# Windowed attention and a softplus FFN: three key chunks folded to two, weights and v in three bfloat16 parts, transposed by DMA, q and k laid transposed

## The chip, the cores and the metric

The kernel runs on one core of one Trainium2 chip. The metric is the device time of one launch in microseconds (us); lower is better. Three runs of the kernel before gave a median of 1070.63 us (1069.97 to 1071.72). The engines are named as in the profile: PE is TensorE (PEld its weight loads), DVE VectorE, ACT ScalarE, POOL GpSimd, SP SyncE, which issues the DMAs.

## The reference, cut to what matters

```python
# q, k, v: (8, 8, 576, 64) float32; w_in (512, 2048), w_out (2048, 512) float64
scores = (1 / sqrt(64)) * q @ k.transpose(0, 1, 3, 2)
rel = pos[:, None] - pos[None, :]
scores = where((rel >= 0) & (rel < 64), scores, -1e9)
attn = exp(scores - max(scores))
attn = attn / (sum(attn) + 1e-9)
x = (attn @ v) as 4608 tokens x 512        # heads side by side
h = x @ w_in
out = ((maximum(h, 0) + log1p(exp(-abs(h)))) @ w_out) as float32
```

Each query sees itself and the 63 keys before it in its own sequence. With 128 queries in a tile, the keys in question are 192: 64 before the tile and the tile's own 128.

## The kernel before, in words

The 4608 tokens are worked in 12 blocks of 384 tokens (TB), which the code counts by g; each block has 3 query tiles of 128 (j) and 4 pairs of heads (hp). One call of `attention(g, hp)` handles one pair of heads of one block and leaves its part of x, transposed, in a high and a low float32r part. The feed-forward part (FFN) handles a block in 16 steps (f), one for each 128 of the 2048 hidden columns: `ffn_up` makes 12 matmuls into a PSUM bank `ps_h` (L450), ACT computes softplus' log term in three instructions (absolute value, exponential, logarithm: L454, L455, L456), DVE adds the positive part (L458) and splits the result into a high and a low part (`g0` at L460, `g1` at L461), and `ffn_down` makes 9 matmuls from them into three banks `ps_o` (L471). Products are made in three passes: high times high, high times low, low times high. In `ffn_down` the first two matmuls of each three read `g0`, the third reads `g1`.

The float64 weights are cut into float32r parts on the chip by `load_w` and `float64_split` (L153 to L174), once, while the first blocks are worked.

For blocks of g >= 2 one call of attention does this. It loads q, k and v in rows. It cuts q and k into three bfloat16 parts (L309 to L313), two in each 128-wide row, which the DMA transposes into `tr` (L314). Per query tile it makes 6 score matmuls of 192 keys (L334), 18 for a pair, adds the mask and takes the row's extreme on DVE (L342), takes the exponential with its sum on ACT (L345), and divides on DVE (L352, L353, L358). PE transposes the 256-wide rows `p_t` in float32 against an identity (L379, L380), two transposes a tile and head. ACT and DVE bring them out of PSUM in two parts (L385, L386). Eight matmuls a head multiply them by v (L427), also in two parts, and ACT and DVE collect `xf` (L431, L432) and split it into x (L139 on DVE, L140 on POOL).

The blocks g = 0 and 1 (`by_pe`) take another way: PE transposes q and k, too, all in float32.

The order of the work is an event list (L497 to L527). Step n of the FFN puts `ffn_up` at place 2n + 0.5 and `ffn_down` at 2n + 3.5, so that one step's down product comes after the next step's up product. The stages of `attention`, which is a generator, get places by the tables STG0, STG2 and STG, the bases BASE, PACE, SH and SHP; from block 3 on a pair of heads comes every 8 places, that is every 4 FFN steps. From place 100 on PE executes in the order of that list. The instructions of ACT, DVE, POOL and SP are ordered by the scheduler at build time; each engine then works its own list strictly from top to bottom.

Of the kernel before, what the change touches and what calls it, by code (L numbers as in the profile page):

```python
# [15 lines left out]
P = 128  # L16
# [3 lines left out]
BIG = 1.0e9  # L20

# [3 lines left out]
PACE = (5, 5, 4)  # L25
STG0 = (-8, 1, 3, 4, 5, 7, 8, 9, 10)
STG2 = (-8, 0, 2, 3, 4, 6, 7, 8, 9)
STG = (-13, -5, 0, 0, 3, 5, 7, 8, 11)
SH, SHP = -5, 8
# [7 lines left out]
def window_attention_softplus_ffn(  # L37
    ctx: ExitStack,
    tc: tile.TileContext,
    q: bass.AP,  # L40
    k: bass.AP,
    v: bass.AP,
    w_in: bass.AP,
    w_out: bass.AP,
    out: bass.AP,
):
# [35 lines left out]
    ident = cpool.tile([P, P], F32, name="ident")  # L82
    make_identity(nc, ident)


    W = WIN + P
    mask = cpool.tile([P, W], BF16, name="mask")
    nc.gpsimd.memset(mask, 0.0)
    nc.gpsimd.affine_select(
        out=mask, in_=mask, pattern=[[1, W]], compare_op=ALU.is_gt, fill=BIG, base=0, channel_multiplier=-1  # L90
    )
    nc.gpsimd.affine_select(
        out=mask, in_=mask, pattern=[[-1, W]], compare_op=ALU.is_ge, fill=BIG, base=WIN, channel_multiplier=1
    )

    mask_b = cpool.tile([P, W], BF16, name="mask_b")
    nc.gpsimd.tensor_copy(mask_b, mask)
    nc.gpsimd.memset(mask_b[WIN:P, 0:P], BIG)

    p_ts = [[cpool.tile([P, NJ, 2 * P], F32, name=f"p_t{i}{hh}") for hh in range(2)] for i in range(2)]  # L100


    NQ, NKB = 2 * NJ, 2 * (NJ + 1)
    NT2 = 2 * (NQ + NKB)
    for t in p_ts[0] + p_ts[1]:
        nc.gpsimd.memset(t[:, :, 0:WIN], 0.0)

# [4 lines left out]
    SPARE = 4 * DM * 4  # L112
# [13 lines left out]
    kbd_s = [spare(k, [P, 2, WIN + TB], F32, f"kbd{k}") for k in range(2)]  # L126
    for t in kbd_s:
        nc.gpsimd.memset(t[D:P, 0, :], 0.0)
        nc.gpsimd.memset(t[0:D, 1, :], 0.0)
    v_pads = []  # L130
    for n in range(2):
        t = spare(6 + n, [P, 2, NJ + 1, 2, P], F32, f"v_pad{n}")
        nc.gpsimd.memset(t, 0.0)
        v_pads += [t[:, i, :, :, :] for i in range(2)]
# [7 lines left out]
    NK = (NJ - 1) * W + P  # L142

    def raw_tiles(f):

        ks = (5,) if f < NE else [k for k in (5,) if k >= 4] if f < NE + 4 else []
        at = f % (len(ks) + 1)
        if at == len(ks):
            return [ff.tile([P, NC, P], w_in.dtype, name="raw", bufs=2) for _ in range(2)]
        t = spare(ks[at], [P, 2, NC, P], w_in.dtype, "raws")  # L150
        return [t[:, m, :, :] for m in range(2)]

    def float64_split(dst_hi, dst_lo, src, raw, n):  # L153


        nc.sync.dma_start(raw, src)
        words = raw.bitcast(U32).rearrange("p c (n two) -> p two c n", two=2)
        low, high = words[:, 0, :, :], words[:, 1, :, :]
        w = ff.tile([P, NC, P], F32, name="osb", bufs=2)
        wb = w.bitcast(U32)  # L160
        nc.scalar.activation(w, high.bitcast(F32), AF.Abs)
        (nc.gpsimd if n < 4 else nc.vector).tensor_scalar(w, w, ZERO_HIGH, None, ALU.max)  # L162
# [3 lines left out]
        nc.scalar.copy(dst_hi, w)  # L166
        nc.gpsimd.tensor_tensor(dst_lo, w, dst_hi.bitcast(F32), ALU.subtract)

    def load_w(f):
        fs = slice(f * P, (f + 1) * P)  # L170
        raws = raw_tiles(f)
        for m, src in enumerate((w_in[:, fs].rearrange("(c p) n -> p c n", p=P), w_out[fs, :].rearrange("p (c n) -> p c n", n=P))):
            hi, lo = [weight(m, i, f).rearrange("p (c n) -> p c n", n=P) for i in range(2)]
            float64_split(hi, lo, src, raws[m], 2 * f + m)  # L174


    def pieces(t0, n):

# [378 lines left out]
```

## Time and profile before

| | |
|---|---|
| median of 3 runs | 1070.63 us |
| the profiled execution's own time | 1069.74 us |
| its span (first to last instruction) | 1067.9 us |
| granted TensorE clock, mean | 0.993 |
| instructions on PE, DVE, ACT, POOL | 6096, 2319, 1669, 217 |
| busy share of the span: PE, PEld, DVE, ACT, POOL | 96%, 87%, 74%, 61%, 21% |
| moved by DMA | 98.20 MB, 92 GB/s on average |

Instruction counts are those of the page, which shows the execution in a span of its own; the profiled execution's time is 1.8 us longer than the span. PE's matmuls are pipelined, so one matmul's listed duration is longer than what it costs in a dense row. What it costs is read from the start of one group to the start of the next in the timeline. The same holds, by some 0.1 us each, for ACT and DVE.

### The profile page before, as it was taken

To read this page: it belongs to the slowest core of one execution; us is meant where nothing else is said; L and a number is where in the kernel's file an instruction comes from. 1 tells how busy PE (TensorE), PEld (TensorE's weight loads), DVE (VectorE), ACT (ScalarE), POOL (GpSimd) and SP (SyncE) were. 2 spreads that over 40 slices of the span, in tenths; PEclk is the share of its full clock that TensorE was granted. 3 is DMA by queue.
4 is the path that set the end of the run, shared out by engine and by line. 5 is a ranking of instruction groups with operands and counts; after the bars stand their busy time and mean duration, and the time that the engine had idled before them with its cause. 6 is when DMAs were issued, how large, how long until landed. Compare 5 with 4: busy or idle time off the path is not lost.

```text
span 1067.9 us, 18172 instructions
## 1 busy us (share of the span) xinstructions
PE 1028.4 (96%) x6096; PEld 924.3 (87%) x6096; DVE 789.0 (74%) x2319; ACT 650.0 (61%) x1669; POOL 224.7 (21%) x217
## 2 busy tenths in 40 slices
PE   7797988999999999999999999999999999999998
PEld 5576867888999899999999999999999999999996
DVE  4999899866777777777777777777777777865433
ACT  6786666666665666566656666656666665655333
POOL 4354355631111111112111111111211111110000
PEclk9999998999999999999999999999999999999999
DMA  7754645255334434343344334424434533520000
GB/s 197 198 140 105 169 105 146 67 127 119 70 71 101 96 79 105 64 97 81 81 96 96 84 76 93 107 60 88 102 74 84 115 80 62 131 51 1 30 1 30
DMA packets 296222, 98.20 MB, mean 92 GB/s; under 512 B 280512, under 2 KB 288704, under 8 KB 296128
## 3 DMA queue, kind: packets, MB, share of 16 engines
q1 hardware_dynamic: 296128, 97.03, 40.0%
q8 instruction: 48, 0.79, 0.3%
q14 instruction: 46, 0.38, 0.1%
HBM read 50.07 MB, written 10.22 MB: 56 GB/s over the span
## 4 chain that ended last, share of the span: by engine, by line
PE 78%; DVE 12%; DMA 4%; ACT 3%; issue 2%; SPq 1%; POOL 0%; DVEq 0%; ACTq 0%
PE ps_h L450 32%; PE ps_o L471 31%; PE ps_a L334 5%; PE ps_a L427 4%; PE ps_a L380 2%; DMA tr<-nat 2%; PE ps_a L379 2%; DVE p_t L358 2%; DVE osb L165 2%; DVE osb L164 1%; DVE osb L162 1%; DVE p_t L342 1%; DVE osb L163 1%; SPq L198 1%; DVE u L458 1%
## 5 line engine op out<-in xcount | busy, mean ns | idle before, releaser
L450 PE MATMUL ps_h<-x,w 128*128 128x384 f32 x2304 | 458.4, 344 | 15.4 <-DVE u L458 11.8
L471 PE MATMUL ps_o<-w,g 128*128 128x512 f32 x1728 | 438.7, 397 | 6.3 <-ACT g L460 4.3
L450 PEld LDWEIGHTS ps_h<-x,w 128*128 128x128 f32 x2304 | 400.6, 189 | 27.5 <-DVE u L458 12.5
L471 PEld LDWEIGHTS ps_o<-w,g 128*128 128x128 f32 x1728 | 318.1, 188 | 65.6 <-ACT g L460 4.6
L458 DVE SCALAR_TENSOR_TENSOR u<-ps_h,u 128x384 f32<-128x384 f32 x192 | 106.0, 552 | 139.7 <-ACT u L456 139.5
L454 ACT ACTIVATE u<-ps_h 128x384 f32<-128x384 f32 x192 | 93.6, 488 | 179.4 <-PE ps_h L450 177.2
L345 ACT ACTIVATE p_t<-p_t,mn 128x192 f32<-128x192 f32 (+1 forms) x288 | 127.0, 443 | 63.5 <-DVE mn L342 63.2
L140 POOL TENSOR_TENSOR x<-xf,x 128x384 fp32r<-128x384 f32 x40 | 41.1, 1027 | 460.6 <-DVE rs L352 362.9
L358 DVE TENSOR_SCALAR p_t<-p_t,rs 128x192 f32<-128x192 f32 (+1 forms) x288 | 110.4, 429 | 2.9
L342 DVE CUSTOM_DVE_ANT_0 p_t<-ps_a,mask 128x192 f32<-128x192 f32 (+1 forms) x244 | 77.3, 343 | 46.5 <-PE ps_a L334 36.1
L455 ACT ACTIVATE u<-u 128x384 f32<-128x384 f32 x192 | 100.7, 526 | 4.1
L456 ACT ACTIVATE u<-u 128x384 f32<-128x384 f32 x192 | 100.6, 524 | 3.2
L461 DVE TENSOR_TENSOR g<-u,g 128x384 fp32r<-128x384 f32 x160 | 89.5, 559 | 3.8 <-DVE g L460 0.5
L385 ACT CAST pt<-ps_a 128x512 fp32r<-128x512 f32 (+1 forms) x144 | 59.0, 417 | 33.7 <-PE ps_a L380 21.9
L312 POOL TENSOR_TENSOR nat<-q_in,nat 128x384 bf16<-128x384 f32 x40 | 38.6, 965 | 187.8 <-ACT nat L311 152.1
L386 DVE TENSOR_TENSOR pt<-ps_a,pt 128x512 fp32r<-128x512 f32 (+1 forms) x144 | 67.9, 477 | 12.3 <-ACT pt L385 10.7
L334 PE MATMUL ps_a<-tr 128*128 128x192 bf16 (+1 forms) x720 | 74.8, 246 | 0.9 <-DVE xf L432 0.7
L460 DVE CAST g<-u 128x384 fp32r<-128x384 f32 x176 | 67.9, 386 | 5.9
L380 PE MATMUL ps_a<-ident,p_t 128*128 128x128 f32 x276 | 66.6, 276 | 1.4 <-DVE p_t L358 1.3
L427 PEld LDWEIGHTS ps_a<-pt,vt 128*128 128x128 f32 (+1 forms) x608 | 64.0, 163 | 3.9 <-issue 0.5
L427 PE MATMUL ps_a<-pt,vt 128*128 128x64 f32 (+4 forms) x608 | 64.5, 247 | 0.4 <-DVE mn L342 0.4
L431 ACT COPY xf<-ps_a 64x384 f32<-64x384 f32 x80 | 38.1, 477 | 40.3 <-PE ps_a L427 37.5
(91 smaller groups left out, 1019.3 us busy)
## 6 DMA issues: line engine op xcount, KB each, us to landing
out_dram<-raw SPq DMA_DIRECT2D x12, 512.0 KB, 3.2
q_in<-in_q_dram SPq DMA_DIRECT2D x56, 96.0 KB, 2.6
raw<-in_moe_w_in_dram SPq DMA_DIRECT2D x10, 512.0 KB, 4.2
raw<-in_moe_w_out_dram SPq DMA_DIRECT2D x10, 512.0 KB, 4.2
k_in<-in_k_dram SPq DMA_DIRECT2D x32, 128.0 KB, 3.5
v_in<-in_v_dram SPq DMA_DIRECT2D x32, 128.0 KB, 2.8
raws<-in_moe_w_in_dram SPq DMA_DIRECT2D x6, 512.0 KB, 4.2
raws<-in_moe_w_out_dram SPq DMA_DIRECT2D x6, 512.0 KB, 5.0
```

Source lines behind the costliest of these rows:

```text
L334: mm(spv[:, hh, :], tr_q[a][:, hh, j * P : (j + 1) * P], tr_k[b][:, hh, kc], start=(hh == 0 and i == 0), stop=(hh == 1 and i == 2), skip_g ...
L342: nc.vector.tensor_tensor_reduce(pv, spv[:, hh, :], m[:, c0:], 1.0, 3.0e38, ALU.add, ALU.min, mn[:, j, hh : hh + 1])
L345: nc.scalar.activation(pv, pv, AF.Exp, bias=mn[:, j, hh : hh + 1], scale=-1.0, accum_out=sm[:, j, hh : hh + 1])
L358: nc.vector.tensor_scalar(pv, pv, rs[:, jj, hh : hh + 1], None, ALU.mult)
L427: mm(av[: D if lo else P, osl], vt[:, vb, hh, : 1 if lo else 2, :], pt[hh][lo][:, psl], start=(i == 0), stop=(i == len(order) - 1), skip_g ...
L450: mm(hv, weight(0, a, f)[:, c * P : (c + 1) * P], x[b][c], start=(i_mm == 0), stop=(i_mm == 3 * NC - 1))
L454: nc.scalar.activation(u, hv, AF.Abs)
L455: nc.scalar.activation(u, u, AF.Exp, scale=-1.0)
L456: nc.scalar.activation(u, u, AF.Ln, bias=1.0)
L458: nc.vector.scalar_tensor_tensor(gf, hv, 0.0, u, ALU.max, ALU.add)
L461: (nc.vector if g >= 2 else nc.gpsimd).tensor_tensor(gt[1], gf, gt[0].bitcast(F32), ALU.subtract)
L471: mm(ops[g][j], gt[a][:, js], weight(1, b, f), start=(first and i == 0), stop=(last and i == 2),)
```

## The change

- The host lays q and k transposed (heads and dimensions in rows, tokens in columns), v by tokens, and the float64 weights by FFN step (`_layouts`). The kernel loads q and k as they are needed; all transposes of q and k go, on PE and by DMA.
- q and k are used as float32r in a high and a low part (L238 to L243). Both halves of the partitions hold the same rows; one half of q's tile carries the high part, the other the low part. A query tile takes 4 score matmuls of 192 keys (L258), 12 for a pair, in place of 18 in bfloat16.
- The scores of a tile stay 192 wide up to the mask (L265). Then the first and the third 64 columns, of which every row has at most one inside its window, are folded into one by a minimum on DVE (L271). All that follows has 128 columns: the exponentials (L275, six in a row), the division (L281, one instruction for all six), the transposes.
- For g >= 2 the attention weights are cut into three bfloat16 parts (L300, L301, L302, L306, L307), which the DMA transposes (L303, L308). PE's 12 transposes for a pair of heads and what brought them out of PSUM go. v is cut into three bfloat16 parts, too (L316 to L320). A head takes 14 matmuls of 64 or 128 columns (L367).
- g = 0 and 1 keep PE's transposes for the weights alone (L288).
- `load_w` handles both weight matrices of a step in one instruction each, 1024 columns wide.
- The stage tables are changed. From block 3 on, the stage that casts q and k for the next pair comes at the place of this pair's first score matmuls, and the stage with all six exponentials and the splits right behind the third.

FFN lines move: `ffn_up`'s matmuls from L450 to L391, its ACT lines from L454, L455, L456 to L395, L396, L397, its DVE lines from L458, L460, L461 to L399, L401, L402; `ffn_down` from L471 to L412.

ACT, the stretch of one pair of heads in the settled part of the program, before. `u` is the FFN step's softplus term, `p_t` the attention weights, `nat` the parts of q and k, `pt` the transposed weights, `xf` attention's output.

```order
L454 ACTIVATE u_6076<-ps_h_6063 128x384
L311 CAST nat_6236<-q_in_6007 128x6x64
L455 ACTIVATE u_6076<-u_6076 128x384
L311 CAST nat_6236<-k_in_6008 128x8x64
L456 ACTIVATE u_6076<-u_6076 128x384
L385 CAST pt10_6051<-ps_a_6094 128x512
L454 ACTIVATE u_6115<-ps_h_6102 128x384
L431 COPY xf_6126<-ps_a_6127 64x384
L455 ACTIVATE u_6115<-u_6115 128x384
L345 ACTIVATE p_t00_101,sm_6137<-p_t00_101,mn_6136 128x128
L345 ACTIVATE p_t01_102,sm_6137<-p_t01_102,mn_6136 128x128
L456 ACTIVATE u_6115<-u_6115 128x384
```

ACT at the same place now. `k0` and `q_hl` are the casts of k and q for the next pair, `st` holds the weights of this pair, `v12` parts of v.

```order
L316 CAST v12_6078<-v_in_5593 128x14x64
L372 COPY xf_6155<-ps_a_6224 64x384
L318 CAST v12_6078<-v_in_5593 128x14x64
L395 ACTIVATE u_6263<-ps_h_6250 128x384
L239 CAST k0_6206<-k_in_6042 128x896
L238 CAST q_hl_6205<-q_in_6041 128x768
L396 ACTIVATE u_6263<-u_6263 128x384
L275 ACTIVATE st_6195,sm_6197<-st_6195,mn_6196 128x128 x6
L397 ACTIVATE u_6263<-u_6263 128x384
L395 ACTIVATE u_6336<-ps_h_6323 128x384
```

Between a step's first and last ACT instruction stood at most two of attention's at a time here; now eight stand inside one step, the casts of k and q and all six exponentials.

DVE, before, around the same FFN step as in ACT's first piece (`mn` and `sm` are the rows' extremes and sums, `rs` the reciprocals):

```order
L352 TENSOR_SCALAR rs_6138<-sm_6137 128x2
L353 RECIPROCAL rs_6138<-rs_6138 128x2
L458 SCALAR_TENSOR_TENSOR u_6115<-ps_h_6102,u_6115 128x384
L358 TENSOR_SCALAR p_t00_101<-p_t00_101,rs_6138 128x128
L358 TENSOR_SCALAR p_t01_102<-p_t01_102,rs_6138 128x128
L460 CAST g0_6120<-u_6115 128x384
L352 TENSOR_SCALAR rs_6138<-sm_6137 128x2
L461 TENSOR_TENSOR g1_6121<-u_6115,g0_6120 128x384
```

DVE, now, around the step `u_6263` of ACT's second piece:

```order
L271 TENSOR_TENSOR st_6195<-st_6195 128x6x64
L243 TENSOR_TENSOR k1_6207<-k_in_6042,k0_6206 128x896
L240 TENSOR_TENSOR q_hl_6205<-q_in_6041,q_hl_6205 64x768
L278 TENSOR_SCALAR sm_6197<-sm_6197 128x6
L279 RECIPROCAL sm_6197<-sm_6197 128x6
L281 TENSOR_TENSOR st_6195<-st_6195,sm_6197 128x6x128
L399 SCALAR_TENSOR_TENSOR u_6263<-ps_h_6250,u_6263 128x384
L401 CAST g0_6268<-u_6263 128x384
L399 SCALAR_TENSOR_TENSOR u_6336<-ps_h_6323,u_6336 128x384
L402 TENSOR_TENSOR g1_6269<-u_6263,g0_6268 128x384
```

The step's own DVE work now stands behind the whole division, which needs the sums of all six exponentials, and its `g1` behind the next step's first DVE instruction.

On PE the order of such a stretch is now, for the four FFN steps A to D of one pair: up A, scores of tile 0, down of the step before; 14 matmuls of the second head of the pair before, scores of tile 1, up B, scores of tile 2, down A; up C, down B; up D, down C; 14 matmuls of the next head. `u_6263` above belongs to B, `u_6336` to C.

The diff, cut to its core:

```diff
-STG = (-13, -5, 0, 0, 3, 5, 7, 8, 11)
-SH, SHP = -5, 8
+STG = (-14, -8, 0, 1, 2, 3, 15, 17)
+SH, SHP = -13, 8
...
+    def load_w(f):
+        if f % 2 and f < NE + 4:
+            raw, w = spare(6, [P, 2, DM], w_words.dtype, "raws"), spare(7, [P, 2, DM], F32, "ws")
+        else:
+            raw = ff.tile([P, 2, DM], w_words.dtype, name="raw", bufs=1)
+            w = ff.tile([P, 2, DM], F32, name="osb", bufs=1)
+        nc.sync.dma_start(raw, w_words[f])
...
+        else:
+            q_in = ld.tile([P, 2, TB], F32, name="q_in")
+            k_in = ld.tile([P, 2, W - P + TB], F32, name="k_in")
+            v_in = ld.tile([P, NCH, P], F32, name="v_in")
+            ts, ks = slice(t0, t0 + TB), slice(t0 - CH, t0 + TB)
+            for half in heads:
+                nc.sync.dma_start(
+                    q_in[half, :, :], qT[c0 : c0 + P, ts].rearrange("(h d) t -> d h t", h=2)
+                )
+                nc.sync.dma_start(
+                    k_in[half, :, :], kT[c0 : c0 + P, ks].rearrange("(h d) t -> d h t", h=2)
+                )
+            for half in heads:
+                nc.sync.dma_start(v_in[half, :, :], v[ks, c0 : c0 + P].rearrange("(c p) n -> p c n", p=CH))
+        yield
         if not by_pe:
+            q_hl = att.tile([P, 2, TB], F32R, name="q_hl")
+            k_hi, k_lo = [att.tile([P, 2, W - P + TB], F32R, name=f"k{i}") for i in range(2)]
+            low = heads[1]
+            nc.scalar.copy(q_hl, q_in)
+            nc.scalar.copy(k_hi, k_in)
+            nc.vector.tensor_tensor(
+                q_hl[low, :, :], q_in[low, :, :], q_hl[low, :, :].bitcast(F32), ALU.subtract
+            )
+            nc.vector.tensor_tensor(k_lo, k_in, k_hi.bitcast(F32), ALU.subtract)
+        yield
...
+                for hh in range(2):
+                    for i, part in enumerate((k_hi, k_lo)):
+                        mm(
+                            spv[:, hh, :], q_hl[:, hh, js], part[:, hh, kc],
+                            start=(hh == 0 and i == 0), stop=(hh == 1 and i == 1), skip_group_check=True,
+                        )
...
+        sv = st.rearrange("p h j c -> p (h j) c")
+        nc.vector.tensor_tensor(sv[:, :, 0:CH], sv[:, :, 0:CH], sv[:, :, P:], ALU.min)
+        for hh in range(2):
+            for j in range(NJ):
+                i = hh * NJ + j
+                nc.scalar.activation(
+                    sv[:, i, 0:P], sv[:, i, 0:P], AF.Exp, bias=mn[:, hh, j : j + 1], scale=-1.0, accum_out=sm[:, i : i + 1]
+                )
+        nc.vector.tensor_scalar(sm, sm, 1.0e-9, None, ALU.add)
+        nc.vector.reciprocal(sm, sm)
+        pn = sv[:, :, 0:P]
+        nc.vector.tensor_tensor(pn, pn, sm.unsqueeze(2).to_broadcast([P, 2 * NJ, P]), ALU.mult)
...
+            nc.scalar.copy(part(0, 0), pv[0])
+            nc.vector.tensor_tensor(pv[0], pv[0], part(0, 0), ALU.subtract)
+            nc.scalar.copy(part(0, 1), pv[0])
+            nc.sync.dma_start(
+                tr[:, 0:n, :], nat[:, 0, :, :, :].rearrange("p n b c -> p (n b c)"), transpose=True
+            )
+            nc.gpsimd.tensor_tensor(part(1, 0), pv[0], part(0, 1), ALU.subtract)
+            nc.vector.tensor_copy(nat[:, 1, :, 1, :], nat[:, 0, :, 0, :])
+            nc.sync.dma_start(
+                tr[:, n:, :], nat[:, 1, :, :, :].rearrange("p n b c -> p (n b c)"), transpose=True
+            )
...
+            nc.scalar.copy(v12[:, :, :, 0, :], vv)
+            nc.vector.tensor_tensor(vv, vv, v12[:, :, :, 0, :], ALU.subtract)
+            nc.scalar.copy(v12[:, :, :, 1, :], vv)
+            nc.gpsimd.tensor_tensor(v13[low, :, :, :], vv[low, :, :, :], v12[low, :, :, 1, :], ALU.subtract)
+            nc.vector.tensor_copy(v13[up, :, :, :], v12[up, :, :, 0, :])
         yield
...
+            for i, (s, c, src, osl) in enumerate(passes):
                 mm(
+                    av[: D if s else P, osl], v13[:, c, hh, :] if s else v12[:, c, hh, :, :], src,
+                    start=(i == 0), stop=(i == len(passes) - 1), skip_group_check=True,
                 )
...
+def _layouts(inputs):
+    got = {n: _np.ascontiguousarray(a.transpose(1, 3, 0, 2).reshape(h * d, b * s)) for n, a in (("qT", q), ("kT", k))}
+    got["v"] = _np.ascontiguousarray(v.transpose(0, 2, 1, 3).reshape(b * s, h * d))
```

More of the change, by code (lines that the diff above doesn't have):

```diff
@@ L20 @@
 BIG = 1.0e9
+CH = 64
+NCH = TB // CH + 1
 SPLIT = 8
@@ L233, in attention @@
     def attention(g, hp):
[L234 removed]
+        c0 = hp * P
         t0 = ORDER[g] * TB
[L236 to L238 removed]
+        prev = t0 % S != 0
+        by_pe = g < 2
         odd0 = g == 0 and hp % 2 == 1
```

405 lines of the change are left out of this document (141 added, 264 removed).

## The prediction

> **What bounds the kernel now.** I read the page's shares and slices first, then the waits of PE in the settled part, then the timelines of SP, PE, ACT and DVE in one stretch of it.
>
> ```profile
> PE 1028.4 (96%) x6096; PEld 924.3 (87%) x6096; DVE 789.0 (74%) x2319; ACT 650.0 (61%) x1669; POOL 224.7 (21%) x217
> PE   7797988999999999999999999999999999999998
> DVE  4999899866777777777777777777777777865433
> ```
>
> Two regimes: for seven or eight slices of 26.7 us PE has holes and DVE is nearly full; from then on PE is full. Busy shares and mean stretches by window (us busy, instructions):
>
> ```profile
> 80.00:100.00 20.00, 14.56 (x66) 11.30 (x64) 19.77 (x40) 13.74 (x35) 9.19 (x8) 0.92 0.57 142
> 372.00:444.00 72.00, 72.00 (x453) 66.43 (x452) 53.52 (x165) 45.28 (x117) 11.64 (x13) 1.00 0.44 95
> ```
>
> The columns are PE, PEld, DVE, ACT, POOL. Early, DVE works 19.77 of 20 us and sets the pace; later PE works 72 of 72. PE's longest wait from 230 to 1040 us:
>
> ```profile
> PE ps_o L471 <- DVE g L460: 0.4, 1, 0.4
> ```
>
> So after 230 us any PE time saved is time saved, as long as the FFN step's way over ACT and DVE stays inside the time that PE gives it. That way is the point of this case. The transposes on SP's queue come once per pair of heads, and give its period, 410.22 - 389.31 = 20.91 us:
>
> ```profile
> 389.31 4.04 SPq L314 DMA_TRANSPOSE tr<-nat  x2
> 410.22 3.76 SPq L314 DMA_TRANSPOSE tr<-nat  x2
> ```
>
> PE in that stretch (start, length, instruction); a group costs the distance to the next one's start:
>
> ```profile
> 398.17 0.27 PE L379 MATMUL ps_a<-ident,p_t 128*128 128x128 f32 x1
> ...
> 398.74 2.33 PE L450 MATMUL ps_h<-x,w 128*128 128x384 f32 x12
> 400.91 0.82 PE L427 MATMUL ps_a<-pt,vt 128*128 128x64 f32 x8
> 401.57 1.16 PE L334 MATMUL ps_a<-tr 128*128 128x192 bf16 x12
> 402.52 2.31 PE L471 MATMUL ps_o<-w,g 128*128 128x512 f32 x9
> 404.67 2.27 PE L450 MATMUL ps_h<-x,w 128*128 128x384 f32 x12
> 406.78 2.24 PE L471 MATMUL ps_o<-w,g 128*128 128x512 f32 x9
> ```
>
> Up costs 2.17 us (398.74 to 400.91) or 2.11 (404.67 to 406.78), down 2.15; six transposes 0.57, so 0.095 each; eight products with v 0.66, so 0.083; twelve scores 0.95, so 0.079.
>
> **PE's work, part by part.** Removed per pair of heads (g >= 2): 18 scores x 0.079 = 1.42, 12 transposes x 0.095 = 1.14, 16 products x 0.083 = 1.32, together 3.88 us. Added: 12 float32r scores of 192 columns. The eight old products are float32r with 1152 columns in all, 0.66 / 1152 x 192 = 0.110 each, so 1.32 us (0.95 if they go at the bfloat16 rows' 0.079). And 28 bfloat16 products of 64 or 128 columns. The nearest row is a bfloat16 group that holds six matmuls of 128 and six of 192:
>
> ```profile
> 526.01 1.00 PE L334 MATMUL ps_a<-tr 128*128 128x128 bf16 x12
> 526.79 2.32 PE L471 MATMUL ps_o<-w,g 128*128 128x512 f32 x9
> ```
>
> 0.78 - 6 x 0.079 = 0.31, so 0.051 each; 28 of them 1.4 us (at most 0.110 each: 3.1; at least 1.0, if the eight of 64 columns cost half and hide). Added 2.7, net -1.2 us per pair, bounds -1.9 and +0.5. [...]
>
> **The way of FFN step B.** Of the four FFN steps in a pair's stretch, PE has between the start of up B and the start of down B: up B 2.17, scores 0.45 (4 x 0.110), down A 2.15, up C 2.11, that is 6.9 us. What has to happen on ACT and DVE in the meantime stands in their orders, and each works its list from the top. ACT:
>
> ```profile
> 396.65 0.47 ACT L454 ACTIVATE u<-ps_h 128x384 f32<-128x384 f32 x1
> 397.03 0.50 ACT L311 CAST nat<-q_in 128x384 bf16<-128x384 f32 x1
> 397.43 0.52 ACT L455 ACTIVATE u<-u 128x384 f32<-128x384 f32 x1
> 397.85 0.60 ACT L311 CAST nat<-k_in 128x512 bf16<-128x512 f32 x1
> 398.36 0.52 ACT L456 ACTIVATE u<-u 128x384 f32<-128x384 f32 x1
> 401.11 0.49 ACT L454 ACTIVATE u<-ps_h 128x384 f32<-128x384 f32 x1 [1.50 <-PE ps_h L450]
> ...
> 402.99 0.45 ACT L345 ACTIVATE p_t<-p_t,mn 128x192 f32<-128x192 f32 x1
> ...
> 403.43 0.45 ACT L345 ACTIVATE p_t<-p_t,mn 128x192 f32<-128x192 f32 x1
> ```
>
> Up started at 398.74, ACT's first instruction on it at 401.11: 2.37 us. A cast of 384 columns holds ACT 0.40 us (397.03 to 397.43), one of 512 0.51 (397.85 to 398.36): 0.86 ns a column. An exponential with its sum takes 0.44 (402.99 to 403.43) for 192 columns, so 0.385 for 128. B's way on ACT: 2.37 until its absolute value starts, 0.38 for that, the cast of k (896 columns) 0.84, of q (768) 0.73, B's exponential 0.42, six exponentials of attention 2.31: 7.05 us, when the slack is already gone. Then DVE:
>
> ```profile
> 391.75 0.16 DVE L352 TENSOR_SCALAR rs<-sm 128x2 f32<-128x2 f32 x1
> 391.94 0.17 DVE L353 RECIPROCAL rs<-rs 128x2 f32<-128x2 f32 x1
> 392.14 1.20 DVE L358 TENSOR_SCALAR p_t<-p_t,rs 128x192 f32<-128x192 f32 x2
> ...
> 396.26 0.56 DVE L310 SCALAR_TENSOR_TENSOR q_in<-q_in,nat 128x384 f32<-128x384 f32 x1 [0.68 <-ACT nat L309]
> 396.73 0.25 DVE L313 COPY nat<-nat 128x384 bf16<-128x384 bf16 x1
> 396.90 0.69 DVE L310 SCALAR_TENSOR_TENSOR k_in<-k_in,nat 128x512 f32<-128x512 f32 x1
> 397.50 0.29 DVE L313 COPY nat<-nat 128x512 bf16<-128x512 bf16 x1
> ...
> 403.86 0.54 DVE L458 SCALAR_TENSOR_TENSOR u<-ps_h,u 128x384 f32<-128x384 f32 x1
> ...
> 404.44 0.36 DVE L460 CAST g<-u 128x384 fp32r<-128x384 f32 x1
> ...
> 404.95 0.55 DVE L461 TENSOR_TENSOR g<-u,g 128x384 fp32r<-128x384 f32 x1
> ```
>
> Two small instructions 0.39 and about 0.1 until the sums arrive; the division, 768 columns on two operands, 0.47 + 384 x 1.02 ns = 0.86 (0.47 for 384 from 396.26 to 396.73, 0.60 for 512); B's add 0.58 until its cast, the cast 0.36. So B's `g0` is ready 7.05 + 0.4 + 0.1 + 0.86 + 0.58 + 0.36 = 9.3 us after up B's start, 2.4 us late. Two more pieces: the second cast of v in front of B waits for a DVE subtraction of 896 columns (1.0 us), which itself waits for the pair before's products and two mask instructions; I get 0.4 us more (0 to 0.8). And `g1` stands behind C's add: 0.27 of the cast, 0.47, 0.55, so 0.9 us behind `g0`, of which two matmuls (0.46) hide half: 0.5. Together PE stalls 3.3 us in down B; I take 3.2 (bounds 2.4 and 3.8). For A, C and D the same sum stays inside: nothing of attention stands between the three ACT instructions of each, and 2.37 + 0.49 + 0.52 + 0.52 + 0.58 + 0.36, by the rows' lengths, is 4.8 us. The pattern stands 29 times in ACT's order; 7 more pairs from block 3 on lack a part of it and count at -1.2 alone.
>
> **The clock.** A stall's second price is the granted clock:
>
> ```profile
> 93.33:96.74 3.41, 0.98 (x4) 0.85 (x5) 3.41 (x13) 3.02 (x10) 2.19 (x2) 1.00 0.65 198
> 96.74:100.15 3.41, 3.15 (x9) 1.94 (x8) 3.38 (x8) 2.76 (x7) 1.06 (x2) 0.50 0.76 215
> 134.29:137.70 3.41, 1.67 (x12) 1.10 (x10) 3.34 (x3) 1.07 (x3) 3.41 (x3) 1.00 0.21 58
> 137.70:141.11 3.41, 2.32 (x12) 2.24 (x13) 3.15 (x10) 2.81 (x7) 2.13 (x3) 1.00 0.38 86
> ```
>
> After a stretch of 3.41 us with 0.98 us of PE work the clock was 0.50 for the next 3.41 us; after one with 1.67 it stayed at 1.00. A stall of 2.8 + 0.5 us leaves less than some 1.3 us of work in one such stretch in about 7 of 10 phases, and half a clock for 3.41 us then costs about 1.4 us: 1.0 us per pair, bounds 0 and 1.7. [...]
>
> **Start, and what hides.** Until some 205 us DVE sets the pace.
>
> ```profile
> L358 DVE TENSOR_SCALAR p_t<-p_t,rs 128x192 f32<-128x192 f32 (+1 forms) x288 | 110.4, 429 | 2.9
> ```
>
> For the eight early pairs six divisions (6 x 0.43) become one of 0.86 and a fold of 0.47, -1.2 each, so -10 us; fewer, wider weight instructions (0.08 us less for each of some 60) save 5, four instructions that come over from POOL and a memset add about 4. I take -10 us; the slices' holes sum to about 40 us, so at best -30, since the first weights have to arrive before any FFN step, at worst +10 if the 1024-column instructions hold up FFN steps there. Folding, splitting and the casts of v hide under PE elsewhere: ACT gets some 1.2 us more per pair, DVE about the same. The transposes of the weights are issued most of a stretch of 20 us before their products; L314's two issues take 4.04 us now, so they cost nothing, and some 4 us a pair only if that distance were gone. On SP's queue the second waits for POOL's subtraction, and behind it stand loads that are read a stretch later.
>
> **Sum,** on the profiled execution's 1069.7 us (0.9 under the median): 29 x (-1.2 + 3.2 + 1.0) = +87, 7 x -1.2 = -8, start -10: 1139 us.
>
> **Rivals.**
> - *The stall does not open* (faster). If casts and exponentials cost ACT and DVE so little that `g0` comes within 6.9 us, 36 x -1.2 and -10 give 1017 us. For it: PE never waits now, and ACT is at 45.28 of 72 us. Against it: the sum would have to be 2.4 us of 9.3 too long, and all its terms are rows. It decides at a stall of 1.8 us, where 29 x (1.8 - 1.2) takes back the 18 us of start and other pairs: below that the kernel is faster. Chance 0.13.
> - *The stall without the clock.* [...] For it: the stretch with 1.67 us. Against it: the one with 0.98. Chance 0.30.
> - *Dear products.* At 0.110 us for each of the 28 the net is +0.5 and the time about 1199 us; the bfloat16 row speaks against it. Chance 0.05.
>
> My forecast has 0.52. The range drops most of the first and the third: 1050 (stall 2.4, no clock, start -30, PE -1.5: 1069.7 + 29 x 0.9 - 41 = 1055) to 1185 (stall 3.8, clock 1.7, start 0: 1069.7 + 29 x 4.3 - 8 = 1186). A measurement of this kernel can tell about 0.2%, 2 us, from no change. Faster 0.14, same 0.03, slower 0.83.
>
> **What would show it.** In the profile after: about 29 waits of PE at L412 for DVE's cast L401, near 3 us each, a pair's period near 24 us, and PEclk at 0.5 behind many of them; up and down groups at 2.1 us as now. Short of the waits, or with another line ahead of them, I am wrong; if they are there and the time is lower, the start or the products are cheaper than I think.

## The result, and the profile after

The changed kernel takes 1280.47 us (median of 4 runs, 1278.76 to 1283.12) against 1071.17 us (4 runs beside it): ratio 1.196, 95% interval 1.193 to 1.198. The profiled execution took 1280.53 us, its span is 1278.7 us. The prediction had the sign and the place right, and the size not: 1139 us, at most 1185.

The page of the changed kernel, busy time and slices of 32 us:

```profile
PE 1092.9 (85%) x5888; PEld 936.3 (73%) x5888; DVE 849.5 (66%) x1764; ACT 690.9 (54%) x1565; POOL 295.5 (23%) x208
PE   6668888799999887888878887888878888889998
DVE  5389997376866677666775667666775666666433
PEclk9668988889999899898988989899898998889999
```

PE is full in slices 9 to 13 alone (256 to 416 us) and near the end. Its waits from 400 to 1150 us (total, times, longest):

```profile
PE ps_o L412 <- DVE g L401: 107.1, 29, 4.1
PE ps_o L412 <- DVE g L402: 2.4, 9, 0.8
```

That is the predicted wait, 29 times, 3.7 us on average (107.1 / 29) instead of 3.2. Of the 3.2 some 2.8 were meant for the first half of g (L401) and the rest for the second (L402), which costs next to nothing here. One stretch, PE's timeline:

```profile
606.98 2.29 PE L391 MATMUL ps_h<-x,w 128*128 128x384 f32 x12
609.11 0.58 PE L258 MATMUL ps_a<-k,q_hl 128*128 128x192 f32 x4
609.53 2.26 PE L412 MATMUL ps_o<-w,g 128*128 128x512 f32 x9
611.63 2.27 PE L391 MATMUL ps_h<-x,w 128*128 128x384 f32 x12
617.67 3.79 PE L412 MATMUL ps_o<-w,g 128*128 128x512 f32 x9 [3.77 <-DVE g L401]
621.29 2.27 PE L391 MATMUL ps_h<-x,w 128*128 128x384 f32 x12
```

Up B starts at 606.98; up C should free PE at 613.7, but down B starts at 617.67 and then costs 3.62 us instead of 2.1. DVE in the same stretch:

```profile
610.30 1.76 DVE L150 CAST x<-xf 128x384 fp32r<-128x384 f32 x1
611.98 0.55 DVE L271 TENSOR_TENSOR st<-st 128x384 f32<-128x384 f32 x1
612.45 1.90 DVE L243 TENSOR_TENSOR k<-k_in,k 128x896 fp32r<-128x896 f32 x1
614.38 0.96 DVE L240 TENSOR_TENSOR q_hl<-q_in,q_hl 64x768 fp32r<-64x768 f32 x1
615.36 0.17 DVE L278 TENSOR_SCALAR sm<-sm 128x6 f32<-128x6 f32 x1
615.57 0.19 DVE L279 RECIPROCAL sm<-sm 128x6 f32<-128x6 f32 x1
615.79 0.96 DVE L281 TENSOR_TENSOR st<-st,sm 128x768 f32<-128x768 f32 x1
616.67 0.55 DVE L399 SCALAR_TENSOR_TENSOR u<-ps_h,u 128x384 f32<-128x384 f32 x1
617.25 0.36 DVE L401 CAST g<-u 128x384 fp32r<-128x384 f32 x1
```

And POOL, with what it waited for in brackets:

```profile
609.93 1.91 POOL L319 TENSOR_TENSOR v<-v_in,v 64x896 bf16<-64x896 f32 x1 [14.48 <-ACT v L318]
612.20 1.20 POOL L151 TENSOR_TENSOR x<-xf,x 128x384 fp32r<-128x384 f32 x1 [0.36 <-DMA tr<-nat]
```

ACT's first exponential of attention and the reading of the sixth sum:

```profile
612.56 0.40 ACT L275 ACTIVATE st<-st,mn 128x128 f32<-128x128 f32 x1 [0.26 <-DVE st L271]
...
614.80 0.19 ACT L275 ACTIVATION_READ_ACCUMULATOR st<-st,mn 128x1 f32 x1
```

The cast of x (L150) takes 1.76 us where L401, the same shape, takes 0.36; it ends 0.2 us after POOL's L319. The subtraction of k (L243) takes 1.90 us, 0.8 more than alone (1.09 in an experiment below), and ends 0.95 us after POOL's L151. Only a part of these 2.2 us reaches PE, because ACT's exponentials run at the same time: the first of them waits 0.26 us for the fold (L271) behind L150, and the sixth sum is there at 614.99, 0.4 us ahead of L278, which stands behind L243 and L240 in DVE's list. By these two figures the waits for POOL lengthen PE's wait by some 0.6 us, an estimate; the rest is the order.

The clock in windows of 3.41 us (PE busy is the second figure, the granted clock the third last):

```profile
610.50:613.92 3.42, 3.40 (x18) 2.87 (x16) 3.42 (x3) 3.16 (x10) 2.54 (x2) 1.00 0.45 93
613.92:617.33 3.41, 0.00 (x0) 0.00 (x0) 3.25 (x7) 3.35 (x11) 0.00 (x0) 1.00 0.64 184
617.33:620.74 3.41, 3.07 (x7) 2.26 (x8) 3.18 (x7) 1.16 (x2) 0.38 (x1) 0.50 0.64 178
620.74:624.15 3.41, 3.41 (x19) 3.15 (x19) 0.00 (x0) 0.52 (x2) 1.39 (x1) 1.00 0.00 0
```

Where the 211 us are, by the start of the same FFN step's up group (us from the span's start; the last two columns are experiments told below):

| up group of step | before | after | v on ACT's queue | combined |
|---|---|---|---|---|
| 0 | 25.4 | 78.1 | 44.4 | 44.6 |
| 24 | 201.2 | 252.7 | 234.1 | 236.0 |
| 52 | 351.3 | 412.0 | 389.2 | 382.6 |
| 164 | 932.8 | 1144.5 | 1121.4 | 951.4 |
| 188 | 1043.3 | 1254.1 | 1230.1 | 1059.2 |

So 61 us are lost up to step 52 and 151 in the 28 stretches from there to step 164: a stretch takes 26.16 us (732.5 / 28) instead of 20.77 (581.5 / 28). By the starts of the groups, averaged over the 28 stretches, what nothing disturbs costs 20.04 us; the wait adds 3.97 (up C's group and the wait behind it take 6.08 instead of 2.11), and what the FFN groups behind it cost beyond their 2.1 us adds 2.15.

### The profile page after: what moved, and what is told of

Read it like the earlier page. It is cut to its first block, busy times and chain, and to the rows that moved or that the text cites. A ratio compares the mean times of both kernels' runs of the same rounds, so it can differ in the third digit from the quotient of the medians.

```text
span 1278.7 us, 17049 instructions
## 1 busy us (share of the span) xinstructions
PE 1092.9 (85%) x5888; PEld 936.3 (73%) x5888; DVE 849.5 (66%) x1764; ACT 690.9 (54%) x1565; POOL 295.5 (23%) x208
## 4 chain that ended last, share of the span: by engine, by line
PE 56%; DVE 30%; issue 6%; DMA 4%; ACT 2%; SPq 1%; DVEq 0%; ACTq 0%
PE ps_o L412 26%; PE ps_h L391 21%; PE ps_a L367 5%; DVE k L243 5%; PE ps_a L258 3%; DVE st L281 3%; DVE st L265 3%; DVE q_hl L240 3%; DVE v_in L317 2%; DVE u L399 2%; DVE st L271 2%; DVE xf L373 1%; DMA raw<-in_w_words_dram 1%; DVE g L401 1%; DMA tr<-nat 1%
## 5 line engine op out<-in xcount | busy, mean ns | idle before, releaser
L412 PE MATMUL ps_o<-w,g 128*128 128x512 f32 x1728 | 487.5, 428 | 121.3 <-DVE g L401 117.5
L412 PEld LDWEIGHTS ps_o<-w,g 128*128 128x128 f32 x1728 | 338.4, 204 | 209.9 <-DVE g L401 121.9
L391 PE MATMUL ps_h<-x,w 128*128 128x384 f32 x2304 | 474.2, 355 | 16.0 <-ACT w L172 10.4
L391 PEld LDWEIGHTS ps_h<-x,w 128*128 128x128 f32 x2304 | 432.8, 201 | 35.4 <-ACT w L172 11.5
L395 ACT ACTIVATE u<-ps_h 128x384 f32<-128x384 f32 x192 | 93.5, 487 | 279.6 <-PE ps_h L391 274.1
L399 DVE SCALAR_TENSOR_TENSOR u<-ps_h,u 128x384 f32<-128x384 f32 x192 | 106.1, 553 | 206.9 <-ACT u L397 206.6
L319 POOL TENSOR_TENSOR v<-v_in,v 64x896 bf16<-64x896 f32 x40 | 78.7, 1968 | 436.7 <-ACT v L318 418.7
L306 POOL TENSOR_TENSOR nat<-st,nat 128x768 bf16<-128x768 f32 x40 | 69.9, 1747 | 262.2 <-ACT nat L302 261.9
L275 ACT ACTIVATE st<-st,mn 128x128 f32<-128x128 f32 x288 | 111.7, 389 | 31.5 <-DVE st L271 31.4
L265 DVE CUSTOM_DVE_ANT_0 st<-ps_a,mask 128x192 f32<-128x192 f32 x216 | 68.4, 354 | 65.9 <-PE ps_a L258 52.5
L396 ACT ACTIVATE u<-u 128x384 f32<-128x384 f32 x192 | 100.4, 525 | 4.4
L397 ACT ACTIVATE u<-u 128x384 f32<-128x384 f32 x192 | 99.7, 521 | 4.4
L402 DVE TENSOR_TENSOR g<-u,g 128x384 fp32r<-128x384 f32 x160 | 91.1, 569 | 9.6 <-DVE g L401 0.5
L367 PEld LDWEIGHTS <-v 128*128 128x128 bf16 (+1 forms) x1088 | 61.9, 105 | 37.4 <-issue 17.7
L258 PE MATMUL ps_a<-k,q_hl 128*128 128x192 f32 x480 | 77.2, 288 | 10.9 <-DVE q_hl L240 6.2
L367 PE MATMUL ps_a<-tr,v 128*64 128x128 bf16 (+3 forms) x1088 | 80.7, 217 | 6.8 <-DMA tr<-nat 5.0
L258 PEld LDWEIGHTS ps_a<-k,q_hl 128*128 128x128 f32 x480 | 69.0, 199 | 14.6 <-DVE q_hl L240 7.0
L401 DVE CAST g<-u 128x384 fp32r<-128x384 f32 x176 | 69.6, 396 | 9.3 <-PE ps_o L412 1.8
L243 DVE TENSOR_TENSOR k<-k_in,k 128x896 fp32r<-128x896 f32 x40 | 68.3, 1707 | 1.9 <-ACT k L239 1.9
L302 ACT CAST nat<-st 128x768 bf16<-128x768 f32 x40 | 33.3, 831 | 54.7 <-DVE st L301 54.6
L150 DVE CAST x<-xf 128x384 fp32r<-128x384 f32 x40 | 56.8, 1419 | 7.9 <-PE ps_h L391 7.7
```

The lines of the kernel that those rows point to most:

```text
L243: nc.vector.tensor_tensor(k_lo, k_in, k_hi.bitcast(F32), ALU.subtract)
L258: mm(spv[:, hh, :], q_hl[:, hh, js], part[:, hh, kc], start=(hh == 0 and i == 0), stop=(hh == 1 and i == 1), skip_group_check=True,)
L265: nc.vector.tensor_tensor_reduce(st[:, hh, j, :], spv[:, hh, :], m, QSCALE, 3.0e38, ALU.add, ALU.min, mn[:, hh, j : j + 1])
L275: nc.scalar.activation(sv[:, i, 0:P], sv[:, i, 0:P], AF.Exp, bias=mn[:, hh, j : j + 1], scale=-1.0, accum_out=sm[:, i : i + 1])
L367: mm(av[: D if s else P, osl], v13[:, c, hh, :] if s else v12[:, c, hh, :, :], src, start=(i == 0), stop=(i == len(passes) - 1), skip_grou ...
L391: mm(hv, weight(0, a, f)[:, c * P : (c + 1) * P], x[b][c], start=(i_mm == 0), stop=(i_mm == 3 * NC - 1))
```

## The experiments

My theory after the result: the wait is made by the order on ACT, lengthened by DVE waiting for POOL; the loss behind the wait is the clock; the start is late because SP's queue issues the weights late. The rivals: DVE is simply full; the loss behind the wait is the second half of g; DVE's pace sets the start. Unless it says otherwise, an experiment is the changed kernel with the edit shown.

### More work in the wait, twice

```diff
+        for again in range(2 if g >= 3 and 55 <= NF * g + f <= 163 and f % 4 == 3 else 1):
             i_mm = 0
             for c in range(NC):
...
```

> In the 28 settled stretches with a long wait, the FFN step in front of the waiting down group does its twelve matmuls of the up projection twice; the second pass writes the same values over the first. PE gets 2.1 us of extra work inside a wait of 3.97 us. If the 2.2 us that PE loses behind each wait are the halved clock, the stretch now holds enough work, the clock stays at 1.00, the wait shrinks to about 1.9 us and the time falls by 28 x 2.2 = 61 us, to about 1219 us, although the kernel works more. If the loss behind the wait has another cause (the second half of g, the bank), the time stays near 1280 us; if the extra work also delays the chain that PE waits for, it goes up by as much as 28 x 2.1 = 59 us, to 1339 us.

1282.27 us: no gain and no loss. PE's timeline at one of the places:

```profile
828.57 0.74 PE L414 MATMUL ps_o<-w,g 128*128 128x512 f32 x2 [1.72 <-DVE g L403]
830.16 2.54 PE L414 MATMUL ps_o<-w,g 128*128 128x512 f32 x7 [0.85 <-DVE g L404]
```

The wait did shrink to some 1.7 us, but at full clock PE reaches the second half of g sooner and waits 0.85 us for it, and the clock is still halved behind 20 of the 28 waits. An unchanged time is what was expected if the loss had another cause than the clock; with a clock that is still halved so often, the run can't tell the two causes apart. So the wait was filled whole, away from anything that ACT reads:

```diff
+        if g >= 3 and 55 <= NF * g + f <= 163 and f % 4 == 3:
+            extra = ps_a.tile([P, 512], F32, name="ps_a")
+            for i in range(20):
+                mm(extra[:, :TB], weight(0, 0, f)[:, 0:P], x[0][i % NC], start=(i == 0), stop=(i == 19))
```

> In the 28 settled stretches with a long wait, PE does 20 more matmuls of 384 columns (3.5 us) into a bank that nobody reads, inside the wait of 3.97 us; the orders on ACT and DVE stay as in the changed kernel. If the 2.2 us lost behind each wait are the halved clock, PEclk is 1.00 throughout the settled part, the down group comes at the same moment and costs its 2.1 us (up to 0.4 us more where it waits for the second half of g): 28 x 1.8 to 2.2 us less, 1219 to 1230 us, with 560 matmuls more. If it is another cost of the wait, the time stays at 1280 us.

1234.22 us: 46 us less with 560 matmuls more, 4 us above the range expected. PEclk on its page, in slices of 31 us, is full from the thirteenth on:

```profile
PEclk7868888989989999999999999999999999999999
```

PE's waits in the down groups (L416 there) from 400 to 1110 us, for the first and the second half of g:

```profile
PE ps_o L416 <- DVE g L405: 10.1, 29, 0.6
PE ps_o L416 <- DVE g L406: 6.3, 29, 0.8
```

0.35 us of the wait are left, and 0.2 us for the second half of g; a stretch takes 24.56 us. So 1.6 of the 2.15 us behind the wait are the clock's price, 28 x (26.16 - 24.56) = 45 us. The rest stays at full clock as well, where the down group costs 2.65 us instead of 2.09 because PE comes to the second half of g before it is ready.

### POOL's subtraction on DVE

```diff
-            nc.gpsimd.tensor_tensor(v13[low, :, :, :], vv[low, :, :, :], v12[low, :, :, 1, :], ALU.subtract)
+            nc.vector.tensor_tensor(v13[low, :, :, :], vv[low, :, :, :], v12[low, :, :, 1, :], ALU.subtract)
```

> The subtraction that makes v's third part (64 x 896) goes from POOL to DVE; by the scheduler's order the logarithm of step B then stands behind three of the six exponentials on ACT, and B's add ahead of the division on DVE. If DVE's cast of x waits until POOL's subtraction ends (1.76 us instead of 0.36), it takes 0.36 us now, and with the new order the first half of g is ready some 2.8 us earlier: the wait falls from 3.97 to about 1.1 us, no clock is halved, and 28 x (2.85 + 2.2) = 141 us go, to about 1140 us. If DVE is simply full there and the cast's length has another cause, the 0.95 us that DVE gets on top lengthen the chain: 1280 to 1310 us.

1208.34 us, 72 less although DVE has 1.1 us more work per stretch, but not the 141 I had worked out. The scheduler also made another order of it: B's add now stands ahead of the division on DVE, so the gain isn't that of POOL's waits alone. DVE in one stretch:

```profile
872.72 0.35 DVE L150 CAST x<-xf 128x384 fp32r<-128x384 f32 x1
873.11 1.09 DVE L319 TENSOR_TENSOR v<-v_in,v 64x896 bf16<-64x896 f32 x1
874.23 1.26 DVE L271 TENSOR_TENSOR st<-st 128x384 f32<-128x384 f32 x1
875.41 1.08 DVE L243 TENSOR_TENSOR k<-k_in,k 128x896 fp32r<-128x896 f32 x1
```

And POOL:

```profile
873.22 1.85 POOL L151 TENSOR_TENSOR x<-xf,x 128x384 fp32r<-128x384 f32 x1 [12.50 <-DVE x L150]
```

The cast is back at 0.35 us, the subtraction of k at 1.08. But POOL's x, which now meets L319 on DVE, takes 1.85 us instead of 1.20, and the fold (L271) waits for it: 1.26 instead of 0.55. The wait is 2.37 us by the groups' starts, not 1.1, and a stretch takes 23.90 us. With x's low half on DVE as well:

```diff
-                split(x_t[0], x_t[1], xf, nc.vector, nc.gpsimd)
+                split(x_t[0], x_t[1], xf, nc.vector, nc.vector)
```

> As the kernel before it, and x's low half (128 x 384) goes from POOL to DVE too. If the subtraction that makes k's low half takes 1.9 us because it waits for POOL's x, it takes 1.0 to 1.1 us now, DVE has 0.5 us more, and the chain is 0.4 us shorter: about 10 us below the kernel with v's third part on DVE alone. If its 1.9 us have another cause (its output's type, ACT reading the same tile), the chain is 0.5 us longer: 15 us above it.

1202.9 us, 5 below the kernel before it (10 expected): the fold takes 0.56 us, L243 1.09, the wait 2.14 us. But a stretch takes 23.94 us, no less than before: the clock is now halved behind all 28 waits instead of 25, and the 5 us come ahead of step 52 (its up group starts at 398.0 us instead of 403.9). The long instructions on DVE were waits for POOL, in whichever instruction they fell; their lengths are no property of type or shape (0.35 and 1.76 us for the one cast, 1.08 and 1.90 for the one subtraction). And 2.14 us of wait remain without any of them, with POOL's two subtractions now in DVE's own list. Whether the order makes these 2.14 us is for the next experiment.

### ACT in the written order

The absolute value, exponential and logarithm of a step stay together, because ACT joins PE among the engines with a written order, and the stage with the exponentials is cut so that the casts of P, v, q and k can be placed.

```diff
-STG = (-14, -8, 0, 1, 2, 3, 15, 17)
+STG = (-14, -3.6, 0, 1, 2, 2.9, 3.6, 4.0, 9.2, 9.6, 15, 17)
-MANUAL = {mybir.EngineType.PE}
+MANUAL = {mybir.EngineType.PE, mybir.EngineType.Activation}
...
+            yield
             nc.scalar.copy(part(0, 1), pv[0])
...
```

> ACT's order in the settled part is the written one instead of the scheduler's: the absolute value, exponential and logarithm of each FFN step stand together, the six exponentials behind those of step B, the casts of k and q behind the six, the two casts of v on both sides of B's three. Nothing is left out and nothing changes engine. If the long wait comes from what stands between B's three instructions on ACT, the wait at the down group of step B goes, the period falls from 26.3 to about 20.1 us and the time to 1105 us (28 x 6.2 less). If POOL's subtraction for v, which now runs beside DVE's making of g, holds DVE up, up to 1.5 us of wait per stretch are left: up to 1147 us. If ACT and DVE have too much work for a stretch, whatever the order, the time stays above 1200 us.

1129.86 us, 151 less. PE's waits at L418 (the down group) from 430 to 1000 us:

```profile
PE ps_o L418 <- DVE g L407: 4.0, 25, 0.3
PE ps_o L418 <- DVE g L408: 2.9, 7, 0.5
```

The 3.69 us (107.1 / 29) have become 0.16 (4.0 / 25), PEclk is full, and a stretch takes 20.83 us (562.4 / 27 from step 56 to 164), about as long as before the change (559.8 / 27 = 20.73). Every instruction is still there on its engine, so DVE and ACT are not simply full. DVE's and POOL's lists changed along with ACT's; that the order makes the wait is shown, that it is ACT's alone is not. What is left of the wait is again POOL, beside B's cast of g (L407) now; DVE, then POOL's subtraction for v (L325):

```profile
700.09 2.08 DVE L407 CAST g<-u 128x384 fp32r<-128x384 f32 x1
```

POOL:

```profile
700.05 1.91 POOL L325 TENSOR_TENSOR v<-v_in,v 64x896 bf16<-64x896 f32 x1 [0.88 <-ACT v L324]
```

### The start: SP's queue

The first four weight loads among the first pairs' loads:

```diff
-            events.append((2 * n - AHEAD, lambda f=f: load_w(f)))
+            events.append((2 * n - AHEAD if f > 3 else -99 + 8 * f, lambda f=f: load_w(f)))
```

> The first four weight loads are asked for among the loads of the first pairs instead of behind all of them; nothing else in the text changes. If the first FFN step is late (78 us, 25 before) because SP's queue issues the first weight load only at 62.9 us, behind 96 small loads, it starts near 45 to 50 us and the time falls by 20 to 40 us, to 1240 to 1260 us. If DVE's pace (19.8 of 20 us busy from 80 to 200) sets the start anyway, the FFN steps behind 100 us stand where they stood and the time stays within 5 us of 1280.

1263.15 us, 17 less, a little short of the 20 to 40 expected of the queue. The first up group starts at 31.5 us instead of 78.1, but most of that is gone by step 24 (240.9 against 252.7). Then block 0's v loads on ACT's queue:

```diff
-                    nc.sync.dma_start(dst, v[s : s + n, c0 : c0 + P].rearrange("p (h d) -> p h d", h=2))
+                    (nc.scalar if g == 0 else nc.sync).dma_start(dst, v[s : s + n, c0 : c0 + P].rearrange("p (h d) -> p h d", h=2))
```

> The eight or nine small loads of v of each of block 0's four pairs are issued by ACT instead of SP; the weight loads keep their place behind the rest of SP's list. SP's list ahead of the first weight load shrinks from 62 to about 40 us, so the first FFN step starts near 55 us (78). If what the queue delays is what the start loses, the time falls by some 20 us; if DVE's pace sets it, by under 10.

1259.4 us, 21 less. SP's first weight load in the changed kernel:

```profile
62.87 0.59 SPq L161 DMA_DIRECT2D raw<-in_w_words_dram  x1
```

And in this one:

```profile
14.11 0.64 SPq L161 DMA_DIRECT2D raw<-in_w_words_dram  x1
```

In the changed kernel 12 small loads, most of some 0.6 us on the queue, for each of eight pairs stand ahead of the first weights, 96 in all. In this one 16 are left: 32 went to ACT's queue, and the scheduler, which was not expected, put the rest behind the first weights. Two ways of issuing the weights earlier bring 17 and 21 us. Both edits together:

> Both: block 0's v loads on ACT's queue and the first four weight loads among the first pairs' loads. First FFN step at 25 to 32 us, as before the change. If SP's queue is what the start loses by, 35 to 55 us less than the changed kernel: 1225 to 1245 us; if a second cause (DVE's in-order list, POOL's subtractions beside it) holds the steps behind 100 us, no more than the 17 us of the early weights alone: 1263 us.

1261.34 us: nothing on top. The queue is worth some 20 us, and something else holds the rest. First suspect, the weight pieces of 1024 columns:

```diff
-        nc.sync.dma_start(raw, w_words[f])
+        for m in range(2):
+            nc.sync.dma_start(raw[:, m, :], w_words[f][:, m, :])
...
+            nc.vector.tensor_scalar(wm, wm, ZERO_HIGH, None, ALU.max)
```

> As the kernel with block 0's v loads on ACT's queue (1259 us), and the weights go through DMA, ACT, DVE and POOL in halves of 512 columns, as before the change, instead of pieces of 1024. If the wide pieces are what the start still loses (DVE's list waits at a weight instruction for a whole piece, and holds the attention behind it), 15 to 35 us less: 1225 to 1245 us. If they are not, the 64 more DVE instructions cost some 5 us: 1259 to 1266 us.

1267.65 us, 8 more: refuted.

### The combined kernel, and what still holds its start

Written order on ACT, v's third part on DVE, block 0's v loads on ACT's queue (the edits above):

> ACT's written order in the settled part, v's third part made on DVE, and block 0's v loads on ACT's queue. If the 2.1 us that B's cast of g still takes with the written order are the wait for POOL's subtraction, they go, the period falls from 20.8 to 20.1 to 20.3 us, and the start brings its 21 us: 1090 to 1100 us. If DVE's own 1.0 us for that subtraction, in front of the second half of g, costs as much, 1105 to 1112 us. Either way it stays above the kernel before, because of the start.

1086.29 us (4 runs, 1084.05 to 1087.28), ratio 1.014 to before, interval 1.012 to 1.016: the best version found, and still slower than the kernel before. From step 56 to 164 a stretch takes 20.32 us (548.7 / 27) against 20.73 before: the change's own gain, 0.4 us. All of the rest is the start: 35 us behind at step 24, 16 at the end. There PE waits in its list for block 2's scores:

```profile
137.57 2.30 PE L258 MATMUL ps_a<-k,q_hl 128*128 128x192 f32 x12 [2.04 <-DVE q_hl L240]
149.73 2.88 PE L258 MATMUL ps_a<-k,q_hl 128*128 128x192 f32 x12 [9.86 <-DVE q_hl L240]
```

So PE's written order was made to begin at step 5 instead of 50 (the first of the two numbers starts PE's order, the second ACT's), and then block 2's attention was written four steps later:

```diff
-PE_ORDERED_FROM = 100
+PE_EARLY, PE_ORDERED_FROM = 10, 100
...
```

> As the combined kernel (1086 us), and PE's written order begins at FFN step 5 instead of step 50, so that block 2's scores stand at steps 12 to 20 in PE's list and not ahead of step 11. If the start's remaining 36 us are PE waiting in its list for those scores (2.0 and 9.9 us for DVE's part of q) with FFN steps behind them that could go, 10 to 25 us less: 1061 to 1076 us. If DVE's pace alone sets it (19.8 of 20 us busy from 140 to 200), within 5 us of 1086.

```diff
-BASE = (-100, -46, 2 * (SPLIT + 16) - 24)
+BASE = (-100, -46, 32)
```

> As the kernel before it, and block 2's attention is written four FFN steps later, where the weights' share of DVE's list is over. If attention of block 2 and the weights collide on DVE, another 5 to 15 us less than the kernel before it. If block 2's first FFN step then waits for its x, 0 to 10 us more.

1117.27 and 1118.29 us, 31 and 32 more. Moving the scores gains nothing: with them out of the way PE waits in the down groups instead (first 340 us of the first of the two):

```profile
PE ps_o L418 <- DVE g L407: 24.0, 9, 5.2
PE ps_a L288 <- DVE st L281: 11.2, 3, 7.6
PE ps_o L418 <- POOL g L408: 9.4, 10, 3.0
```

The scheduler's mixed order was better than the written one there. Is it that DVE has more work? One window each, from 8 us to the down group of step 24, DVE's busy time being the fourth figure. The kernel before:

```profile
8.00:219.00 211.00, 181.41 (x974) 150.88 (x974) 194.71 (x493) 144.46 (x375) 97.25 (x79) 0.97 0.55 143
```

The changed kernel:

```profile
8.00:271.00 263.00, 200.78 (x979) 168.29 (x979) 193.27 (x362) 137.71 (x334) 102.90 (x75) 0.84 0.46 129
```

The combined kernel:

```profile
8.00:248.00 240.00, 188.51 (x967) 160.40 (x966) 188.61 (x359) 135.91 (x329) 92.82 (x70) 0.84 0.50 140
```

DVE has much the same work in all three (195, 193 and 189 us) and idles 16, 70 and 51 us of it all: 53 and 35 us more idling, less 1 and 6 us of work, are the delays of that down group, 52 and 29 us. So it is not more work on DVE. That DVE's waits are the cause does not follow, because work and idling of any engine fill the window: PE idles 33 and 22 us more and is busy for 19 and 7 more. Its clock is 0.84 in both, against 0.97 before, and no run here prices that part. The largest of DVE's waits, which was the next suspect, is in the combined kernel the one for a pair's six sums:

```profile
DVE sm L278 <- ACT st L275: 16.6, 5, 7.7
```

Before the change it was 1.4 us in four waits. Hence the last experiment, fold, exponentials, sums and division by head in the first eight pairs:

```diff
+        for r in (slice(0, NJ), slice(NJ, 2 * NJ)) if by_pe else (slice(0, 2 * NJ),):
-        nc.vector.tensor_tensor(sv[:, :, 0:CH], sv[:, :, 0:CH], sv[:, :, P:], ALU.min)
+            nc.vector.tensor_tensor(sv[:, r, 0:CH], sv[:, r, 0:CH], sv[:, r, P:], ALU.min)
...
```

> As the combined kernel (1086 us), and in the first eight pairs fold, exponentials, sums and division are done for each head by itself (three tiles at a time) instead of for both together; every value is the same. DVE idles 48.7 us until step 24 in the combined kernel (14.3 us before the change), 16.6 of them in front of the first instruction on the six sums. If that chain, made long by folding three chunks to two and dividing in one piece, is what the start still loses, the idle time there falls below 8 us and the time by 8 to 15 us, to 1071 to 1078 us. If DVE then only waits at the next instruction for PE or ACT, the 32 more DVE instructions cost up to 8 us: 1086 to 1094 us.

1100.91 us, 15 more. The run hardly tests the sums, because the wait for them falls only from 16.6 to 13.3 us, and the one for the weights' absolute value rises from 3.4 to 14.3. DVE's list, put together anew, waits elsewhere. What holds the start back by some 35 us at step 24, beyond the queue, stays open: three edits, aimed at the width of the weight pieces, PE's scores of block 2 and the six sums, each made the kernel slower (by 8, 31 and 15 us).

## Why the prediction was right and wrong

- *What bounds, and where the wait opens:* right. PE waits at L412 for L401, once per stretch, for the predicted reason: what stands inside step B on ACT, and behind it on DVE. Another order with the same instructions removes it (3.69 to 0.16 us).
- *PE's net, -1.2 us:* the undisturbed groups sum to 20.04 us against 20.77, -0.7. The products' term was mis-sized: 0.90 us for 14, 0.064 each, where I took 0.051 from a mixed bfloat16 group; the scores came out at 1.37 us for 1.32. Inside the bounds.
- *The wait, 3.2 us:* 3.97, and that for the first half of g alone, for which I had some 2.8. `g0` was to free down B 9.7 us after up B's start (9.3 and 0.4 for the casts of v); it came after 10.7, and PE's own groups in front cost 6.75 us instead of 6.9. The failed step is that I counted DVE only from the sums on. Ahead of them it had L150 and L243 in its list, and both waited for POOL, 1.4 and 0.8 us longer than their widths say, of which some 0.6 us reached PE. I had the rows to see it: a cast of the same shape (L460) at 0.36 and at up to 1.4 us in the trace of before. The 0.5 us for the second half of g came to 0.08 a stretch (2.4 / 29), because PE at half clock comes to it late.
- *The clock, 1.0 us:* 2.15 behind the wait, 1.6 of it the clock's own price by the filled wait, 45 us in all. The failed step is the share of phases: I let the clock be halved in 7 of 10 for one window of 3.41 us; it was halved behind all 28 waits, for two windows behind 11 of them. The wait of 4 us is longer than a window.
- *The start, -10 us:* +61. The failed step is the sentence that DVE sets the pace there. I priced DVE's instructions, and not the issues on SP: 96 small loads ahead of the first weights. That is some 20 of the 61 us. DVE's work hardly changed (193.27 us against 194.71 up to step 24); it idles 70 us instead of 16. Why it does, and so the cause of the other 40 us, stays open.
- *Sum:* 28 x (-0.73 + 3.97 + 2.15) = 151 us and 61, against 87 - 8 - 10. Stretches and start have about half of the error of 141 us each.
- *Rivals:* "the stall does not open" and "the stall without the clock" (1069.7 + 29 x (3.2 - 1.2) - 18 = 1110 us) are out by the waits and PEclk, "dear products" by 0.064 us each. The clock was halved behind the window shown above (0.00 us of work, then 0.50), and behind others of the 28 with up to 1.51 us, below.

## What to carry to other kernels

When a change shifts work between engines, cost the whole in-order list in front of the instruction that PE waits for, on every engine it passes, and count a DVE cast or subtraction between SBUF tiles that meets a running POOL instruction as done only behind that instruction's end (here 0.22 us behind it for the cast of x, 0.95 for the subtraction of k). Count issues as well as bytes on a DMA queue: here the first weight load was issued at 62.87 us behind 96 small loads and at 14.11 behind 16, 0.61 us for each of the 80. A wait on PE costs more than its length where the clock is halved behind it: here 3.97 us cost 2.15 more and 2.14 us still 1.76 more, but 0.3 us, with the clock left at full, only 0.2. So between these kernels the first 1.8 us off the wait were worth 2.2 a stretch and the next 1.8 were worth 3.1.

## What the runs showed of the hardware

- **DVE's cast of x and subtraction of k waited for POOL's instruction to end.** The cast takes 0.36 us with POOL idle and 1.75 to 1.77 in 28 of its 40 cases, beside POOL's L319; the 32 casts that start while L319 runs all end 0.22 us behind its end. The subtraction of k takes 1.09 and 1.90; the 28 that start while POOL's L151 runs end 0.94 to 0.95 us behind its end. It goes the other way, too: beside DVE's L319 POOL's own L151 goes from 1.20 to 1.85, and ends 0.87 us behind it. The masked scores (L265), which read PSUM, do not change: 0.34 to 0.36 us in the 51 cases in which a POOL instruction runs from before their start to behind their end, 0.34 to 0.36 with POOL idle.
- **The clock was halved behind windows in which PE worked 1.51 us of 3.41.** In the changed kernel the 28 stretches at half clock from 400 to 1150 us lasted 3.41 us (17) or 6.83 (11), so the work is counted here in windows of 3.41 us, with their successors. In the kernel with both subtractions on DVE, 1.45 us of PE work, then a clock of 0.50:

```profile
870.35:873.76 3.41, 1.45 (x8) 0.89 (x6) 3.31 (x7) 3.35 (x14) 0.00 (x0) 1.00 0.87 215
873.76:877.17 3.41, 3.41 (x9) 2.68 (x9) 3.26 (x7) 1.54 (x3) 0.00 (x0) 0.50 0.69 170
```

In the one with v's alone, 1.55 us, then 1.00:

```profile
994.50:997.91 3.41, 1.55 (x9) 1.23 (x7) 3.31 (x5) 2.64 (x12) 0.32 (x1) 1.00 0.73 189
997.91:1001.33 3.42, 3.07 (x14) 2.45 (x15) 3.27 (x8) 2.45 (x6) 0.00 (x0) 1.00 0.89 239
```

Behind 400 us in the changed kernel, the busiest window ahead of a halving had 1.51 us of work (637.81 to 641.22) and the least busy that kept the clock 1.53 (1030.34 to 1033.76), 0.44 and 0.45 of the window. The border is no constant of all work: with the up group done twice a window with some 1.73 us (827.74 to 831.15) was followed by half the clock, and in the start of the kernel before one with 1.73 us (25.06 to 28.47) was, too, while one with 1.67 (134.29 to 137.70) was not.
- **Extra matmuls were free, and more.** 560 of them in PE's wait made the kernel 46 us faster (1234.22 us for 1280.47).
